# A third relu buffer, a single scratch for the maxima, and normalisations moved between the first value tiles, in a fused attention and MLP block

## The chip, the cores and the metric

One core of one Trainium2 chip runs the whole program as one launch. The metric is device time in microseconds; lower is better. A core has five engines with a queue each: TensorE (PE, its weight loads shown as PEld), VectorE (DVE), ScalarE (ACT), GpSimd (POOL) and SyncE (SP), which here only issues DMA transfers. Each engine works its queue in order, and engines wait for one another at semaphores.

## The reference

The input `x` has 2048 rows of 640. One normalisation feeds both an attention with a sliding window and an MLP with a squared relu; the MLP gates the attention.

```python
def _A_ref(x, wqkv, wo):
    H = 32; Dh = D // H; W = 256
    q, k, v = ...                      # x @ wqkv, split into 32 heads of 20
    scores = jnp.einsum("bhqd,bhkd->bhqk", q, k) * (Dh ** -0.5)
    mask = (idx[:, None] - idx[None, :] >= 0) & (idx[:, None] - idx[None, :] < W)
    p = _softmax(jnp.where(mask[None, None], scores, -1e9), axis=-1)
    o = jnp.einsum("bhqk,bhkd->bhqd", p, v)
    return o.transpose(...).reshape(B, S, D) @ wo

def _B_ref(x, w1, b1, w2, b2):         # 640 -> 1536 -> 640
    h = jnp.einsum("bsd,df->bsf", x, w1) + b1
    r = jnp.where(h > 0, h, 0)
    return jnp.einsum("bsf,fd->bsd", r * r, w2) + b2

xn = _layernorm(A_x)
return A_x + _A_ref(xn, A_wqkv, A_wo) * _silu(_B_ref(xn, ...))
```

## The kernel before, in words

Every number that is multiplied is carried as a high part and a rest ("split"), so most products are three matmuls that accumulate in one PSUM tile, and ScalarE and VectorE make the two parts.

**First phase** (about the first 117 us). The rows are worked in four blocks of 512 (four tiles of 128). For each block the x tiles are loaded on SP (`load_x`), VectorE takes mean and variance (`stats`), ScalarE takes the root and VectorE the reciprocal (`inv_std`, L146 and L147), and VectorE normalises each tile (`normalize`, L151). TensorE turns the normalised tiles (`transpose_chunks`, L167); the first heads' queries and keys and all values are multiplied out of the result. `v_all(b)` makes the values of block `b`: for each half `nh` of the 640 columns and each of four row tiles `t`, TensorE adds 15 matmuls (L230) into a tile of the pool `pmm`, which has three; ScalarE copies the high part (L254), VectorE subtracts it (L255, into `r1`, which has two buffers), and the `rest` (L258 on ScalarE, L259 on VectorE) follows one tile later. Between the two halves `next_x` turns the next block's x, and for later blocks the statistics and normalisations run as `jobs` inside `v_all`. For block 0 the order is different: the second block's normalisations and eleven transfers (the x tiles of the third block, the two spills of the first block's turned x, both biases, the ones rows and the raw weights of the second head group) stand ahead of `v_all(0)`. The order within each engine is the order in which the code calls them: the phase is under a manual schedule, as is the rest.

**Attention and MLP** (about 117 to 830 us). The loop runs 268 steps; 256 of them are one query tile of one of 16 pairs of heads. `scores` multiplies queries and keys for the pair's two heads (L439, into the PSUM tag `s`, two buffers), and `maxima` (L451) adds the mask and takes the row maximum on VectorE: one instruction for each head, whose full-size result goes into a scratch tile `junk` that nothing reads, and whose maximum goes into `mt`, read out by an accumulator instruction of its own. Every fourth step the maxima become rows (L455, L456, a turn on TensorE at L465, a copy at L469) that join the queries. Nine steps later `scores_t` (L483), `exps` (L490 on ScalarE, the window cut by POOL at L491 and L493), `high` (L498) and `low` (L504, `pl`) make the probabilities, and `values` (L518) multiplies them with the values. Between these pieces `fill` feeds TensorE with the remaining queries and keys and the MLP, planned by estimated costs. `flush` runs what the fillers left over: for each of 96 half chunks of the MLP, `half(h)` takes the relu of one half of the PSUM tile `hps` into `r` on ScalarE (L806), squares it there for the high part (L807), and lets VectorE multiply the same half of `hps` with `r` (L809, into `sq`) and POOL subtract (L810). `half(0)` runs at one flush and `half(1)` at the next. `at2` is the pool of `junk` and `r`, two buffers by default.

**The end** (about 830 us on) turns the attention's output, multiplies it with `wo` and combines it with the gate and the input.

Of the kernel before, what the change touches and what calls it, by code (L numbers as in the profile page):

```python
# [7 lines left out]
F32 = mybir.dt.float32  # L8
F32R = mybir.dt.float32r
BF16 = mybir.dt.bfloat16  # L10
# [4 lines left out]
P = 128  # L15
# [6 lines left out]
KC = D // P  # L22
# [9 lines left out]
MT = 256  # L32
# [19 lines left out]
def attn_mlp_kernel(ctx: ExitStack, tc, x, wqkv, wo, w1, b1, w2, b2, out):  # L52
# [62 lines left out]
    def ones_rows(i):  # L115
        nc.sync.dma_start(ks[i][KR:KR + 2].rearrange("a h (c n) -> a (h c) n", n=2 * P), ones.unsqueeze(1).to_broadcast([2, S // P, 2 * P]))
# [10 lines left out]
    with tc.tile_pool(name="ph1v", bufs=2) as p1v, tc.tile_pool(name="ph1", bufs=2) as p1, tc.tile_pool(name="ph1x", bufs=4) as p1b, tc.tile_pool(name="ph1w", bufs=1) as p1w:  # L127
        xts = {}

        def load_x(b, upto=4):  # L130
            xts.setdefault(b, [])
            for t in range(len(xts[b]), upto):
                xt = p1b.tile([P, D], F32, tag="xt", name=f"xt_{b}_{t}")
                nc.sync.dma_start(xt, x[(4 * b + t) * P:(4 * b + t + 1) * P, :])
                xts[b].append(xt)
# [9 lines left out]
        def inv_std(rstd, var):  # L145
            nc.scalar.activation(rstd, var, AF.Sqrt, bias=eps)  # L146
            nc.vector.reciprocal(rstd, rstd)  # L147

        def normalize(xt, mv, rstd):
            xn = p1b.tile([P, D], F32, tag="xn", name="xn")  # L150
            nc.vector.tensor_scalar(xn, xt, mv[:, 0:1], rstd, ALU.subtract, ALU.mult)  # L151
            return xn
# [5 lines left out]
        def spill_x(b):  # L158
            for p in range(2):
                nc.sync.dma_start(xs_d[p][b], f32(xT[p][b]))  # L160
# [9 lines left out]
        def load_w(raw_src, shape3=None):  # L170
            raw = wgt.tile([P, D], F32, tag="wraw", bufs=RAW, name="raw")
            if shape3:
                raw = raw.rearrange("p (c n) -> p c n", c=shape3)
            nc.sync.dma_start(raw, raw_src)
            return raw
# [53 lines left out]
            for m, (xp, wp, c) in enumerate(mms):  # L229
                nc.tensor.matmul(ps, xT[xp][b][:, c * BT + t * P: c * BT + (t + 1) * P], wv[wp][:, c, nh * HALF:(nh + 1) * HALF], start=first and m == 0, stop=not first and m == len(mms) - 1)  # L230

        def v_all(b, between=None):
            late = []
            jobs = norm_jobs(b + 2) if b + 2 < NB else []
            for nh in range(2):
                if nh and between:
                    between()
                vt = p1v.tile([P, NP // 2, 4, 2, VW], BF16, tag="vt", name="vt")
                nc.gpsimd.memset(vt[:, :, :, :, VW - 1:VW], 1.0)
                ahead = 2 if between and not nh else 1  # L240
                pss = []
                for t in range(4):
                    if t in (0, ahead) or t > ahead:
                        ts = range(t, max(t + 1, ahead))
                        for t_ in ts:
                            pss.append(pmm.tile([P, HALF], F32, tag="mm", name="vps"))
                            v_part(pss[-1], b, t_, nh, [(xp, wp, c) for c in range(KC) for xp, wp in ((0, 0), (1, 0))], True)
                        for t_, ps in zip(ts, pss):
                            v_part(ps, b, t_, nh, [(0, 1, c) for c in range(KC)], False)
                    ps = pss.pop(0)  # L250
                    psv = ps.rearrange("p (a h d) -> p a h d", a=NP // 2, h=2)
                    dst = vt[:, :, t, :, :]
                    r1 = p1.tile([P, NP // 2, 2, DH], F32, tag="r1", name="r1")
                    nc.scalar.activation(dst[:, :, :, 0:DH], psv, AF.Copy)  # L254
                    nc.vector.tensor_sub(r1, psv, dst[:, :, :, 0:DH])  # L255

                    def rest(dst=dst, r1=r1):
                        nc.scalar.activation(dst[:, :, :, DH:2 * DH], r1, AF.Copy)  # L258
                        nc.vector.tensor_sub(dst[:, :, :, 2 * DH:3 * DH], r1, dst[:, :, :, DH:2 * DH])  # L259
                    if late:  # L260
                        late.pop()()
                    late.append(rest)
                    for _ in range(0 if between and not nh else 2 if between else 1):
                        if jobs:
                            jobs.pop(0)()
                    store_all()
                late.pop()()
                stores.append((v_d[:, nh * (NP // 2):(nh + 1) * (NP // 2), b, :], vt.rearrange("p a t h w -> p a (t h w)")))

        E_ = mybir.EngineType  # L270
        with tc.manual_schedule(engines={E_.PE, E_.Activation, E_.DVE, E_.Pool, E_.SP}):
# [103 lines left out]
            for b in range(NB):  # L375
                def next_x():
                    if b + 1 < NB:
                        alloc_x(b + 1)
                        transpose_chunks(b + 1, xns)
                        xns.clear()  # L380
                        store_all()
                        spill_x(b + 1)

                if b == 0:
                    inv_std(rstd1, mv1[:, :, 1])
                    xns = [normalize(xts[1][t], mv1[:, t, :], rstd1[:, t:t + 1]) for t in range(4)]
                    load_x(2)
                    spill_x(0)
                    nc.sync.dma_start(b1t, b1.rearrange("(c p) -> p c", p=P))
                    nc.sync.dma_start(b2t, b2.partition_broadcast(P))  # L390
                    ones_rows(0)
                    raws = [load_w(group_src(1, w), KC) for w in "qk"]
                    v_all(b, next_x)
                    continue
                lasts = []
                for w in "kq":
                    ps = pmm.tile([P, BT], F32, tag="mm", name="qkps")
                    qk_group(w, b, ps)
                    lasts.append(qk_evac(w, b, ps))
                for f in lasts:  # L400
                    f()
                next_x()
                if b == 1:
                    for w in "qk":
                        ws1[w] = group_tiles(1, w)
                        split_w(*ws1[w], raws.pop(0))
                if b == NB - 1:
                    store_all()
                    for half in range(2):
                        for dst, src in pair_loads(0, half):  # L410
                            nc.sync.dma_start(dst, src)
                v_all(b)
# [32 lines left out]
    def maxima(p, q, r, nk):  # L445
        if q % 4 == 0:
            mts[p, q // 4] = at2.tile([P, 2, 4], F32, tag="mt", name="mt")
        mt = mts[p, q // 4]
        for hh in range(2):
            junk = at2.tile([P, 3 * P], BF16, tag="junk", name="junk")  # L450
            nc.vector.tensor_tensor_reduce(out=junk[:, :nk], in0=r[hh][:, :nk], in1=mask[:, 3 * P - nk:], scale=1.0, scalar=-3.0e38, op0=ALU.add, op1=ALU.max, accum_out=mt[:, hh, q % 4:q % 4 + 1])  # L451
        if q % 4 == 3:

            mp = mps[q // 4 % 2][:, 0:16].rearrange("p (h a b) -> p h a b", h=2, a=2)
            nc.vector.tensor_scalar(mp[:, :, 0, :], mt, -1.0, None, ALU.mult)  # L455
            nc.vector.scalar_tensor_tensor(mp[:, :, 1, :], mt, -1.0, mp[:, :, 0, :], ALU.mult, ALU.subtract)  # L456
            mts[p, q // 4] = mps[q // 4 % 2]
# [272 lines left out]
    def filler():  # L730
# [51 lines left out]
        for n, (hf, b) in enumerate(blocks):  # L782
# [12 lines left out]
            for fc in range(NFH):  # L795
                ps = pmm.tile([P, BT], F32, tag="mm", name="hps")
                yield from mm_group(ps, [(lin1(wt1, (wp * KC + c) * FHALF + fc * P, P), xb[xp][:, c * BT:(c + 1) * BT]) for c in range(KC) for wp, xp in ((0, 0), (0, 1), (1, 0))], 0.213)
                hh = [stg.tile([P, BT], F32R, tag="stg", name="hh"),
                      stg.tile([P, BT], F32R, tag="stg", name="hl") if fc < NFH - 4 else wgt.tile([P, D], F32R, tag=f"wg{'kq'[fc % 2]}l", name="hl")[:, :BT]]
                hs.append(hh)  # L800

                def evac(ps=ps, hh=hh, fi=hf * NFH + fc):
                    def half(h):
                        sl = slice(h * MT, (h + 1) * MT)
                        r = at2.tile([P, MT], F32, tag="relu", name="relu")
                        nc.scalar.activation(r, ps[:, sl], AF.Relu, bias=b1t[:, fi:fi + 1])  # L806
                        nc.scalar.activation(hh[0][:, sl], r, AF.Square)  # L807
                        sq = at2.tile([P, MT], F32, tag="sq", name="sq")
                        nc.vector.scalar_tensor_tensor(sq, ps[:, sl], b1t[:, fi:fi + 1], r, ALU.add, ALU.mult)  # L809
                        nc.gpsimd.tensor_sub(hh[1][:, sl], sq, f32(hh[0][:, sl]))  # L810
                    half(0)
                    late.append(lambda: half(1))
                pending.append(evac)
# [254 lines left out]
```

## Time and profile before

| | |
|---|---|
| median of 3 runs | 920.18 us (920.01 to 920.91) |
| profiled execution | 920.92 us, of which 919.2 us from the first instruction to the last |
| granted TensorE clock | 0.999 |
| busy: PE, PEld, DVE, ACT, POOL | 901.6, 728.5, 752.9, 668.6, 535.2 us |

Busy times are unions over the span, so an engine at 98% of 919.2 us is hardly ever without an instruction; matmuls overlap and their ends are modelled, so that alone doesn't say that TensorE is at its peak. The chain of waits is followed back from the last instruction: at each step to whatever released it, or to the instruction before it on the same engine. In lists in order of time, each row has the start in us from the span's start, the length, the engine and line, and in square brackets how long the engine had been idle and who released it; idle times under 0.15 us are not named there.

### The profile page before, as it was taken

The numbers are of one execution on the slowest core, as the hardware profiler recorded it, in microseconds if no ns is written. First come the engines' busy times: TensorE is split into PE (matmuls) and PEld (weight loads), VectorE is DVE, ScalarE is ACT, GpSimd is POOL, SyncE is SP. The second block draws the span as 40 slices with busy tenths as digits, with TensorE's granted clock in tenths as the row PEclk, the third lists the DMA queues.
The fourth block names the chain that finished last, engine by engine and source line by source line (L and its number), as shares of the span: only waits on it lengthen the run. The fifth ranks groups of instructions, "written<-read, shape, count | busy, mean of one in ns | idle before, by whom it ended". The sixth has DMA issues, their size and how long they took to land.

```text
span 919.2 us, 21779 instructions
## 1 busy us (share of the span) xinstructions
PE 901.6 (98%) x7632; PEld 728.5 (79%) x7632; DVE 752.9 (82%) x2031; ACT 668.6 (73%) x1282; POOL 535.2 (58%) x832
## 2 busy tenths in 40 slices
PE   9999999999999999999999999999999999999998
PEld 8999976666666678688688788678788687789998
DVE  7875478989899988988888989987888988875654
ACT  5454339888988986987986988977987977994221
POOL 6010017887778885775765877875864965872000
PEclk9999999999999999999999999999999999999999
DMA  6899786677877453253255144365174264055873
GB/s 240 287 396 333 219 264 203 220 221 233 266 232 243 134 197 98 88 182 119 70 184 166 53 123 151 102 226 158 51 252 134 74 208 145 19 191 188 285 276 115
DMA packets 130803, 168.79 MB, mean 184 GB/s; under 512 B 44100, under 2 KB 91268, under 8 KB 128132
## 3 DMA queue, kind: packets, MB, share of 16 engines
q1 hardware_dynamic: 130692, 167.39, 56.2%
q8 instruction: 60, 0.98, 0.4%
q14 instruction: 51, 0.42, 0.1%
HBM read 96.15 MB, written 70.91 MB: 182 GB/s over the span
## 4 chain that ended last, share of the span: by engine, by line
PE 76%; DVE 12%; ACT 5%; issue 3%; POOL 3%; DMA 1%; DVEq 0%; POOLq 0%; SPq 0%; ACTq 0%
PE yps L851 16%; PE hps L569 14%; PE wops L569 8%; PE vps L230 7%; PE ops L518 7%; PE stps L483 7%; PE sps L439 7%; PE qkps L569 6%; DVE junk L451 3%; DVE pl L504 3%; PE qkps L200 2%; ACT p L490 2%; DVE w L672 1%; ACT ph L498 1%; PE otp L917 1%
## 5 line engine op out<-in xcount | busy, mean ns | idle before, releaser
L490 ACT ACTIVATE p<-stps,ebias 128x384 f32<-128x384 f32 (+2 forms) x512 | 258.3, 557 | 80.7 <-PE stps L483 67.3
L451 DVE CUSTOM_DVE_ANT_0 junk<-sps,mask 128x384 bf16<-128x384 f32 (+2 forms) x512 | 250.9, 526 | 59.1 <-PE sps L439 51.9
L504 DVE TENSOR_TENSOR pl<-p,ph 128x768 f16<-128x768 f32 (+2 forms) x256 | 243.1, 950 | 3.4 <-ACT ph L498 3.3
L491 POOL TENSOR_SCALAR_AFFINE_SELECT p<-p 128x256 f32<-128x256 f32 x256 | 146.1, 571 | 127.7 <-ACT p L490 117.5
L498 ACT ACTIVATE ph<-p 128x768 f16<-128x768 f32 (+2 forms) x256 | 206.0, 805 | 14.1 <-POOL p L493 11.7
L569 PE MATMUL hps<-xb,w 128*128 128x512 f32 x630 | 198.2, 430 | 0.0
L851 PE MATMUL yps<-w,hh 128*128 128x320 f32 x768 | 197.6, 330 | 0.0
L851 PEld LDWEIGHTS yps<-w,hh 128*128 128x128 f32 x768 | 132.2, 189 | 7.8 <-issue 1.6
L569 PEld LDWEIGHTS hps<-xb,w 128*128 128x128 f32 x630 | 113.3, 189 | 21.5 <-issue 0.7
L439 PE MATMUL sps<-ks,qs 120*128 120x384 bf16 (+2 forms) x512 | 127.5, 319 | 2.4 <-DVE mt L451 1.9
L483 PE MATMUL stps<-qs,ks 122*128 122x384 bf16 (+2 forms) x512 | 124.5, 322 | 3.6 <-ACT p L490 1.9
L851 PE MATMUL yps<-w,hl 128*128 128x320 f32 x384 | 126.6, 330 | 0.0
L810 POOL TENSOR_TENSOR hl<-sq,hh 128x256 fp32r<-128x256 f32 x96 | 102.6, 1070 | 37.4 <-DVE sq L809 25.2
L493 POOL TENSOR_SCALAR_AFFINE_SELECT p<-p 128x256 f32<-128x256 f32 x224 | 112.4, 502 | 0.0
L518 PEld LDWEIGHTS <-ph 128*128 128x128 f16 x1440 | 86.0, 97 | 26.4 <-issue 21.5
L518 PE MATMUL ops<-vp,ph 128*128 128x61 bf16 x1440 | 101.0, 192 | 0.0
L518 PE MATMUL ops<-vp,pl 128*128 128x61 bf16 x1440 | 99.7, 191 | 0.0
L518 PEld LDWEIGHTS <-pl 128*128 128x128 f16 x1440 | 87.8, 97 | 0.0
L851 PEld LDWEIGHTS yps<-w,hl 128*128 128x128 f32 x384 | 72.4, 189 | 4.6 <-issue 1.5
L483 PEld LDWEIGHTS <-ks 122*128 122x128 bf16 x512 | 30.0, 99 | 56.4 <-issue 44.9
L230 PE MATMUL vps<-wv,xT 128*128 128x320 f32 x480 | 71.7, 308 | 0.6 <-DVE r L255 0.6
L230 PEld LDWEIGHTS vps<-wv,xT 128*128 128x128 f32 x480 | 70.5, 188 | 0.9 <-DVE r L255 0.9
(116 smaller groups left out, 1476.9 us busy)
## 6 DMA issues: line engine op xcount, KB each, us to landing
ks<-k_d SPq DMA_DIRECT2D x64, 240.0 KB
qs<-q_d SPq DMA_DIRECT2D x64, 240.0 KB
xb<-xs SPq DMA_DIRECT2D x12, 1280.0 KB
xs<-xT SPq DMA_DIRECT2D x8, 1280.0 KB
y<-ysb SPq DMA_DIRECT2D x32, 320.0 KB
q_d<-shm SPq DMA_DIRECT2D x38, 256.0 KB
v_d<-vt SPq DMA_DIRECT2D x8, 976.0 KB
vp<-v_d SPq DMA_DIRECT2D x16, 488.0 KB
```

The source lines that it names most:

```text
L230: nc.tensor.matmul(ps, xT[xp][b][:, c * BT + t * P: c * BT + (t + 1) * P], wv[wp][:, c, nh * HALF:(nh + 1) * HALF], start=first and m == 0 ...
L439: nc.tensor.matmul(ps[:, :nk], qs[i][0:KR, hh, q * P:(q + 1) * P], ks[i][0:KR, hh, k0 * P:k0 * P + nk], start=True, stop=True)
L451: nc.vector.tensor_tensor_reduce(out=junk[:, :nk], in0=r[hh][:, :nk], in1=mask[:, 3 * P - nk:], scale=1.0, scalar=-3.0e38, op0=ALU.add, op ...
L483: nc.tensor.matmul(ps[:, :n], ks[i][0:KR + 2, hh, kb * P:(kb + 1) * P], qs[i][0:KR + 2, hh, kb * P:kb * P + n], start=True, stop=True)
L490: nc.scalar.activation(p32[:, hh, :n], r[hh][:, :n], AF.Exp, scale=SCALE, bias=ebias)
L491: nc.gpsimd.affine_select(p32[:, :, 0:P], p32[:, :, 0:P], pattern=[[0, 2], [1, P]], compare_op=ALU.is_ge, fill=0.0, base=0, channel_multip ...
L493: nc.gpsimd.affine_select(p32[:, :, 2 * P:], p32[:, :, 2 * P:], pattern=[[0, 2], [-1, P]], compare_op=ALU.is_gt, fill=0.0, base=0, channel ...
L498: nc.scalar.activation(ph[:, :, :n], p32[:, :, :n], AF.Copy)
L504: nc.vector.tensor_sub(pl[:, :, :n], p32[:, :, :n], ph[:, :, :n])
L518: nc.tensor.matmul(ot[:, q % 4, hh, :], t[:, hh, (q - k) * P:(q - k + 1) * P], vp[:, k // 4, k % 4, hh, :], start=m == 1, stop=m == 2 * le ...
L569: nc.tensor.matmul(ps, a, b_, start=j == 0, stop=j == n - 1)
L851: nc.tensor.matmul(pss[nh], hs[fc][hp][:, tt * P:(tt + 1) * P], lin1(wt2, (wp * NFH + fc) * D + nh * HALF, HALF), start=fc == 0 and j == 0 ...
```

## The change

Three edits. The scratch `junk` of the maxima gets one buffer instead of two. The relu `r` gets three instead of two. And in block 0 the second block's normalisations no longer stand ahead of `v_all(0)`: the root, the reciprocal and the first two tiles come behind the first value tile's copy and subtraction, the third tile behind the second value tile's, and the fourth, with the eleven transfers, behind the third's.

```diff
-        def v_all(b, between=None):
+        def v_all(b, between=None, firsts=()):
...
                     if late:
                         late.pop()()
                     late.append(rest)
+                    if not nh and t < len(firsts):
+                        firsts[t]()
...
                 if b == 0:
-                    inv_std(rstd1, mv1[:, :, 1])
-                    xns = [normalize(xts[1][t], mv1[:, t, :], rstd1[:, t:t + 1]) for t in range(4)]
-                    load_x(2)
-                    spill_x(0)
-                    nc.sync.dma_start(b1t, b1.rearrange("(c p) -> p c", p=P))
-                    nc.sync.dma_start(b2t, b2.partition_broadcast(P))
-                    ones_rows(0)
-                    raws = [load_w(group_src(1, w), KC) for w in "qk"]
-                    v_all(b, next_x)
+                    xns, raws = [], []
+
+                    def norm1(t0, n):
+                        if t0 == 0:
+                            inv_std(rstd1, mv1[:, :, 1])
+                        for t in range(t0, t0 + n):
+                            xns.append(normalize(xts[1][t], mv1[:, t, :], rstd1[:, t:t + 1]))
+
+                    def loads1():
+                        load_x(2)
+                        spill_x(0)
+                        nc.sync.dma_start(b1t, b1.rearrange("(c p) -> p c", p=P))
+                        nc.sync.dma_start(b2t, b2.partition_broadcast(P))
+                        ones_rows(0)
+                        raws.extend(load_w(group_src(1, w), KC) for w in "qk")
+                    v_all(b, next_x, [lambda: norm1(0, 2), lambda: norm1(2, 1), lambda: (norm1(3, 1), loads1())])
                     continue
...
-            junk = at2.tile([P, 3 * P], BF16, tag="junk", name="junk")
+            junk = at2.tile([P, 3 * P], BF16, tag="junk", bufs=1, name="junk")
...
-                        r = at2.tile([P, MT], F32, tag="relu", name="relu")
+                        r = at2.tile([P, MT], F32, tag="relu", bufs=3, name="relu")
```

## The prediction

> **What bounds the kernel now.** First the page: which engine is full, and through what the chain of work that ended last runs.
>
> ```profile
> PE 901.6 (98%) x7632; PEld 728.5 (79%) x7632; DVE 752.9 (82%) x2031; ACT 668.6 (73%) x1282; POOL 535.2 (58%) x832
> PE 76%; DVE 12%; ACT 5%; issue 3%; POOL 3%; DMA 1%; DVEq 0%; POOLq 0%; SPq 0%; ACTq 0%
> ```
>
> TensorE sets the time over most of the span, but 12% of the chain is VectorE. Second view: how the chain splits by line (the head of the chain listed in order of time), and the row of the maxima, L451, in the view of their tile.
>
> ```profile
> by line: PE yps L851 16.3%; PE hps L569 13.7%; PE wops L569 7.7%; PE vps L230 7.0%; PE ops L518 6.8%; PE stps L483 6.7%; PE sps L439 6.6%; PE qkps L569 6.5%; DVE junk L451 3.5%; DVE pl L504 2.8%; issue 2.7%; PE qkps L200 2.5%; ACT p L490 1.
> L451 DVE CUSTOM_DVE_ANT_0 junk<-sps,mask x512: 275/552/561, 119.5 to 806.9; 128x384 bf16<-128x384 f32 x149, 128x128 bf16<-128x128 f32 x11, 128x256 bf16<-128x256 f32 x11
> ```
>
> The maxima are 512 instructions, a pair for each of 256 attention steps. 3.5% of 919.2 us is 32 us of them on the chain. The steps lie in 806.9 - 119.5 = 687 us, so one step is 2.69 us and a stretch of 25 us has 9.3 of them. Third view: busy time by engine in stretches of 25 us (columns: stretch, length, PE, PEld, DVE, ACT, POOL busy). The first eight are the attention stretches where VectorE has least room; the ninth is the fullest of all others.
>
> ```profile
> 142.00:167.00 25.00, 25.00 (x196) 17.37 (x195) 23.34 (x66) 22.14 (x41) 19.44 (x27) 1.00 0.68 210
> 167.00:192.00 25.00, 24.24 (x209) 16.53 (x208) 23.79 (x61) 21.65 (x42) 21.06 (x29) 1.00 0.68 216
> 217.00:242.00 25.00, 23.64 (x209) 16.20 (x208) 23.30 (x61) 21.02 (x40) 19.71 (x29) 1.00 0.76 233
> 242.00:267.00 25.00, 24.59 (x208) 16.90 (x204) 23.63 (x63) 23.11 (x43) 19.31 (x29) 1.00 0.78 242
> 267.00:292.00 25.00, 23.96 (x208) 16.36 (x208) 24.56 (x60) 21.82 (x41) 20.71 (x28) 1.00 0.67 210
> 292.00:317.00 25.00, 23.27 (x199) 15.63 (x196) 24.86 (x65) 22.47 (x45) 20.29 (x27) 1.00 0.58 174
> 542.00:567.00 25.00, 24.69 (x251) 21.64 (x251) 24.86 (x68) 19.82 (x35) 18.24 (x27) 1.00 0.58 166
> 567.00:592.00 25.00, 24.83 (x216) 17.09 (x215) 23.66 (x67) 23.40 (x48) 19.36 (x28) 1.00 0.40 120
> ...
> 717.00:742.00 25.00, 24.98 (x216) 18.30 (x213) 22.84 (x64) 23.27 (x48) 23.46 (x36) 1.00 0.34 100
> ```
>
> In three of them (24.56, 24.86, 24.86) VectorE is full and TensorE is not: there VectorE sets the pace, and what is added to it is added to the kernel. The granted clock is 1.00 in all of them, so no term below comes from the clock.
>
> **Edit 1: one scratch buffer for the maxima.** Nothing is added to compute; `junk` is written and never read. With two buffers the two heads of a step write different ones. With one, the second head's maxima overwrites the first's, and the order of two writes to one buffer has to be kept by a wait of VectorE for itself. What the pair looks like now (start, length):
>
> ```profile
> 401.23 0.55 DVE L451 CUSTOM_DVE_ANT_0 junk<-sps,mask 128x384 bf16<-128x384 f32 x1
> 401.70 0.08 DVE L451 DVE_READ_ACCUMULATOR2_ANT mt<- 128x1 f32 x1
> 401.70 0.55 DVE L451 CUSTOM_DVE_ANT_0 junk<-sps,mask 128x384 bf16<-128x384 f32 x1
> ```
>
> The second starts 0.08 us before the first has ended (401.78): unordered neighbours overlap. What a wait of VectorE for its own last instruction costs is seen where a buffer already comes round. First the chain of waits at `srt`, which has two buffers: its third writer follows the first one's reader, L211.
>
> ```profile
> 19.56 0.65 DVE slo L211
> 20.21 0.03 issue
> 20.24 0.02 DVEq L207
> 20.26 0.05 issue
> 20.31 0.43 DVE srt L207
> ```
>
> 0.10 us pass from the end of L211 to the start of L207, with an item of VectorE's sequencer (DVEq) between. The same for `r1`, two buffers, third writer L255 behind the first one's reader L259; ScalarE's input was there at 26.90.
>
> ```profile
> 26.47 0.43 ACT L254 ACTIVATE vt<-vps 128x320 bf16<-128x320 f32 x1
> 26.60 0.50 DVE L259 TENSOR_TENSOR vt<-r,vt 128x320 bf16<-128x320 f32 x1 [0.15 <-ACT vt L258]
> 27.20 0.49 DVE L255 TENSOR_TENSOR r<-vps,vt 128x320 f32<-128x320 f32 x1
> ```
>
> Again 0.10 us (27.10 to 27.20). Both instructions have a second thing to wait for, as a maxima has (its scores). The cheaper form, one wait alone, is L455 behind the maxima:
>
> ```profile
> 406.65 0.09 DVE L451 DVE_READ_ACCUMULATOR2_ANT mt<- 128x1 f32 x1
> 406.76 0.17 DVE L455 TENSOR_SCALAR mp<-mt 128x8 bf16<-128x8 f32 x1
> ```
>
> 0.02 us here. So a pair grows by 0.08 of lost overlap plus 0.10, that is 0.18 us; the lower end with a wait is 0.08 + 0.02, taken as 0.11 with the 0.01 of rounding; the lowest is nothing, if no wait is set. A gain is excluded: the instructions stay the same. I take 0.18, since the maxima has two waits like L207 and L255. The first maxima of a step would wait for the second one of the step before, but `pl` (L504) and more lie between, so that wait is met when it is reached: nothing. Behind the waiting instruction on VectorE stand `mp`, the copy of the rows, the splits and `pl`; TensorE waits for the scores' bank that a maxima frees and for `mp`.
>
> How much of 0.18 x 256 = 46 us shows? Where TensorE paces, the step has room and it is hidden; that cover ends where VectorE's busy time nears the full stretch. From below: 32 us of maxima on the chain are 31 pairs of 1.02 us (twice 0.55 less the overlap of 0.08), and 31 x 0.18 = 5.6 us are added to a chain that can only get longer. By stretches: each gets 9.3 x 0.18 = 1.67 us more, and what then exceeds 24.6 of 25 (the least of the three full ones) prolongs it, by 1.67 at most: 0.4, 0.9, 0.4, 0.7, 1.6, 1.7, 1.7, 0.7, in the order of the rows, 8.0 us with the hundredths. The ninth row comes to 24.5 and stays hidden. I take 8.0, because it also counts stretches that fill up only by the change; ends 0 and 46.
>
> **Edit 2: a third buffer for the relu.** No instruction is added or removed. ScalarE writes `r` (L806), then reads it (L807); VectorE reads it (L809). All that a further buffer could take away is ScalarE's wait for L809:
>
> ```profile
> ACT relu L806 <- DVE sq L809: 1.7, 6, 0.5
> 330.92 0.47 ACT L806 ACTIVATE relu<-hps,b1t 128x256 f32<-128x256 f32 x1
> 331.82 0.48 DVE L809 SCALAR_TENSOR_TENSOR sq<-hps,b1t,relu 128x256 f32<-128x256 f32 x1
> 332.34 0.47 ACT L806 ACTIVATE relu<-hps,b1t 128x256 f32<-128x256 f32 x1 [0.50 <-DVE sq L809]
> ```
>
> 1.7 us in six waits. But look at whom the second L806 waits for: the L809 that ends at 332.30 reads the half before, which sits in the other of two buffers. The buffer that is written at 332.34 was last read a whole chunk earlier. So the buffer is not what it waits for; what both share is the tile `hps`, of which each reads its half. I take 0, ends 0 and -1.7. The Trainium skill, "PSUM — Partial Sum Buffer", section "PSUM bank collisions raise a hardware error", says that ScalarE and VectorE must not read one bank at the same time and that compilers therefore order any two such accesses. By that rule the wait stays with any number of buffers (0), by the buffer reading 1.7 us go; the row fits the rule.
>
> **Edit 3: the second block's normalisations between the first value tiles.** Moved: one root (L146) on ScalarE, one reciprocal and four L151 on VectorE, and on SP eleven transfers (four x tiles, two spills, both biases, the ones rows, two raw weights). POOL gets and loses nothing.
>
> ```profile
> 22.98 0.81 ACT L254 ACTIVATE vt<-vps 128x320 bf16<-128x320 f32 x2
> 23.47 2.18 DVE L151 TENSOR_SCALAR xn<-xt,mv,rstd 128x640 f32<-128x640 f32 x4
> 25.57 0.88 DVE L255 TENSOR_TENSOR r<-vps,vt 128x320 f32<-128x320 f32 x2
> 18.73 6.76 PE L230 MATMUL vps<-wv,xT 128*128 128x320 f32 x45
> 26.11 2.47 PE L230 MATMUL vps<-wv,xT 128*128 128x320 f32 x15 [0.61 <-DVE r L255]
> 28.42 2.34 PE L167 MATMUL tps<-ident,xn 128*128 128x128 f32 x20
> 26.94 1.81 SPq L134 DMA_DIRECT2D xt<-in_A_x_dram  x4
> 39.41 1.80 SPq L174 DMA_DIRECT2D raw<-in_A_wqkv_dram  x2
> 50.80 0.77 ACT L178 ACTIVATE wgqh<-raw 128x640 fp32r<-128x640 f32 x1
> ```
>
> TensorE stands for 0.61 us before the fourth value tile, since the first tile's bank is freed by an L255 that queues behind all four L151. Now the first L255 can go once its L254 is through, at about 23.3, and ends about 23.8, long before TensorE needs the bank at 25.49: the gap goes, -0.6. What is late next: the transposes need the last L151. VectorE from 23.8: reciprocal 0.2, two L151 1.1, L255 0.5, L259 0.5, L151 0.6, L255 and L259 1.0 gives the last L151 from about 27.1 to 27.7; TensorE ends the fourth tile at 25.49 + 2.3 = 27.8. Just covered; should it be late by some tenths, the gap comes back in front of L167, so -0.6 to 0. SP: the x loads start at 26.94 behind stores; the last of four needs its buffer from the last L151 and would go at 26.94 + 3 x 0.45 = 28.3, later than 27.7, so nothing shifts, and the raw weights issued at 39.41 are not split before 50.80. From 26.11 to the end of this phase TensorE runs without such a gap, so 0.6 us arrives at the end. I take -0.6.
>
> **Sum.** +8.0 + 0 - 0.6 = +7.4 us. The profiled execution took 920.92 us (span 919.2, the rest around it 1.7), 0.74 above the median of 920.18. On the profiled one: 928.3; for the median 927.6, which I give.
>
> **The rivals.** *The order costs nothing.* Either no wait is set for two writes on one in-order engine, or it is free. Then only -0.6 is left: 919.6, no change. For it: 225 of the 256 pairs are not on the chain; against it, the two gaps of 0.10 us above. It decides from a price per pair of about 0.08 us down: 9.3 x 0.08 = 0.74 in each of the three full stretches is 2.2, and with -0.6 it stays under 1.8. The Trainium skill, "VectorE: DVE Perf Modes", section "The DRAIN you can't avoid", has measured that a semaphore after every copy "costs nothing extra", because the next instruction waits for the pipe anyway; by it 919.6 comes out here. This trace disagrees: neighbours start 0.08 us before the end, waiting ones 0.10 after.
>
> *The cheap wait.* 0.11 us a pair, 1.02 a stretch: the same eight rows give 0, 0.2, 0, 0.1, 1.0, 1.0, 1.0, 0.1, in all 3.4, less 0.6: 923.0.
>
> *The relu pays and the maxima don't.* -1.7 - 0.6 from edits 2 and 3, place: ScalarE's six waits in the MLP chunks: 917.9. Against it: whom L806 waits for, and that ScalarE is 5% of the chain.
>
> *The wait is paid everywhere.* If the scores' banks and `mp` come late in every step, up to 46 - 0.6: 965.6. Against it: outside the eight stretches VectorE has 2.2 us or more of room in 25, by the ninth row.
>
> **How the numbers follow.** Forecast (925 to 936) 0.55; cheap wait (922 to 925) 0.20; no cost (918.4 to 922) 0.13; faster 0.04; paid far more widely (above 936) 0.08. About 0.2%, 1.8 us, is what a measurement of this kernel can tell from no change; so slower 0.83, same 0.13, faster 0.04. The range takes in the no-cost case and leaves out the last two: 919.4 to 936. The likeliest case has 925 to 936 for itself.
>
> **What would show it.** In the changed trace the pair's starts lie 0.65 us apart instead of 0.47 (0.58 with the cheap wait, 0.47 with none); stretches around 270 to 320 and 545 to 570 grow while those where TensorE paces keep their step of about 2.7 us; L806 still waits for L809 about six times; and TensorE's row at 26.11 has lost its 0.61. The prediction falls if the pair's starts stay at 0.47, or if TensorE's slack takes in more than I gave it.

## The result and the profile after

The changed kernel takes 934.23 us (median of 6 runs, 933.95 to 935.24) against 920.17 us before (6 runs, 919.87 to 920.91): ratio 1.0152, 95% interval 1.0142 to 1.0162. It is 14.1 us slower, where +7.4 was predicted. The profiled execution has a span of 932.5 us at a granted clock of 1.00.

The page of the kernel after: the span, the engines' busy times, and the shares of its chain by engine.

```profile
span 932.5 us, 22164 instructions
PE 904.7 (97%) x7632; PEld 729.2 (78%) x7632; DVE 767.8 (82%) x2031; ACT 671.0 (72%) x1282; POOL 541.7 (58%) x832
PE 52%; DVE 7%; ACT 4%; issue 2%; POOL 1%; DMA 0%; SPq 0%; DVEq 0%; POOLq 0%; ACTq 0%
```

The instructions are as many as before on every engine. The chain's shares sum to 66%: it breaks off in the middle of the attention, so nothing is read from it here. VectorE's timeline of one pair of maxima (start, length):

```profile
283.98 0.55 DVE L460 CUSTOM_DVE_ANT_0 junk<-sps,mask 128x384 bf16<-128x384 f32 x1
284.46 0.08 DVE L460 DVE_READ_ACCUMULATOR2_ANT mt<- 128x1 f32 x1
284.68 0.56 DVE L460 CUSTOM_DVE_ANT_0 junk<-sps,mask 128x384 bf16<-128x384 f32 x1
```

The starts lie 0.70 us apart, not 0.48 as before. The first pair member is over at 284.54 with its accumulator read, the second starts 0.14 later. The view of the maxima's line has one more new row (length least/median/most in ns): items of VectorE's own sequencer. Before there were four of them:

```profile
L451 DVEq EVENT_SEMAPHORE  x4: 50/50/232, 118.9 to 119.2; - x4
```

After:

```profile
L460 DVEq EVENT_SEMAPHORE  x389: 21/21/234, 118.5 to 820.0; - x195
```

Each of the 256 second maxima now has such an item ahead of it. The other 133 belong to first maxima and, all but two, are over 0.3 us or more before these start (1.25 us, median), so they hold nothing up.

Over all 256 pairs the mean distance of the starts is 0.684 us after and 0.455 before: the price of the wait is 0.229 us. Next the views of waits (who waits for whom: us in total, times, longest). Before:

```profile
DVE junk L451 <- PE sps L439: 51.9, 89, 1.8
PE sps L465 <- DVE mp L456: 3.6, 6, 1.5
PE sps L439 <- DVE mt L451: 1.9, 8, 0.6
```

After:

```profile
DVE junk L460 <- PE sps L448: 23.7, 49, 1.6
PE sps L448 <- DVE mt L460: 10.3, 23, 1.0
PE sps L474 <- DVE mp L465: 6.3, 11, 1.5
ACT relu L815 <- DVE sq L818: 4.3, 7, 1.1
```

VectorE's waiting for scores halves (28 us less), and TensorE stands 8.4 us longer before the next scores, whose bank a maxima has to free, and 2.7 us longer before the turned maxima. Last the busy times by stretch. The 256 steps fall into four stretches: steps 0 to 87, 88 to 151, 152 to 183 and 184 to 255 (columns as in the prediction). Before:

```profile
120.00:355.00 235.00, 228.63 (x1871) 161.70 (x1869) 214.72 (x578) 196.66 (x362) 175.24 (x247) 1.00 0.70 217
355.00:526.00 171.00, 170.80 (x1580) 133.24 (x1577) 146.75 (x436) 139.59 (x272) 117.73 (x200) 1.00 0.39 124
526.00:616.00 90.00, 87.31 (x803) 68.41 (x802) 83.52 (x233) 78.23 (x150) 70.45 (x102) 1.00 0.47 141
616.00:806.00 190.00, 189.98 (x1745) 148.87 (x1744) 162.18 (x482) 154.23 (x301) 130.91 (x222) 1.00 0.42 133
```

After, the same steps:

```profile
119.00:363.00 244.00, 231.15 (x1875) 162.87 (x1874) 219.59 (x582) 198.22 (x362) 175.71 (x248) 1.00 0.67 209
363.00:534.00 171.00, 170.90 (x1577) 133.07 (x1576) 149.94 (x436) 139.75 (x272) 122.05 (x199) 1.00 0.40 124
534.00:629.00 95.00, 88.28 (x803) 68.39 (x801) 87.59 (x232) 78.16 (x148) 67.83 (x103) 1.00 0.45 138
629.00:819.00 190.00, 189.62 (x1742) 148.53 (x1741) 165.63 (x481) 154.61 (x300) 134.69 (x219) 1.00 0.42 130
```

The reader is to see the first two numbers of each row. In the second and the fourth stretch TensorE was busy all the time before (0.2 us idle in 361), and these stretches keep their length although each of their pairs is longer. In the first and the third TensorE already stood for 6.4 and 2.7 us, and these two grow by about 8 and 5 us. Measured from the ends of the second maxima, the growth is 8.1, -0.1, 5.2 and 0.3 us. The third number of each row marks the same two stretches: before, VectorE was busy for 91% and 93% of them, for 86% and 85% of the others.

### The profile page after: what moved, and what is told of

The parts are those of the page before. It is cut to its first block, busy times and chain, and to the rows that moved or that the text cites. A ratio compares the mean times of both kernels' runs of the same rounds, so it can differ in the third digit from the quotient of the medians.

```text
span 932.5 us, 22164 instructions
## 1 busy us (share of the span) xinstructions
PE 904.7 (97%) x7632; PEld 729.2 (78%) x7632; DVE 767.8 (82%) x2031; ACT 671.0 (72%) x1282; POOL 541.7 (58%) x832
## 4 chain that ended last, share of the span: by engine, by line
PE 52%; DVE 7%; ACT 4%; issue 2%; POOL 1%; DMA 0%; SPq 0%; DVEq 0%; POOLq 0%; ACTq 0%
PE yps L860 15%; PE hps L578 12%; PE wops L578 8%; PE ops L527 5%; PE stps L492 5%; PE sps L448 5%; DVE pl L513 2%; DVE junk L460 2%; ACT p L499 1%; DVE w L681 1%; ACT ph L507 1%; PE otp L926 1%; DVE sq L818 1%; ACT relu L815 1%; POOL p L500 0%
## 5 line engine op out<-in xcount | busy, mean ns | idle before, releaser
L460 DVE CUSTOM_DVE_ANT_0 junk<-sps,mask 128x384 bf16<-128x384 f32 (+2 forms) x512 | 270.7, 529 | 65.0 <-PE sps L448 23.7
L500 POOL TENSOR_SCALAR_AFFINE_SELECT p<-p 128x256 f32<-128x256 f32 x256 | 157.1, 614 | 121.5 <-ACT p L499 105.1
L819 POOL TENSOR_TENSOR hl<-sq,hh 128x256 fp32r<-128x256 f32 x96 | 105.7, 1102 | 43.8 <-DVE sq L818 29.7
L502 POOL TENSOR_SCALAR_AFFINE_SELECT p<-p 128x256 f32<-128x256 f32 x224 | 107.0, 478 | 0.0
```

The costliest lines, as they stand in the source:

```text
L500: nc.gpsimd.affine_select(p32[:, :, 0:P], p32[:, :, 0:P], pattern=[[0, 2], [1, P]], compare_op=ALU.is_ge, fill=0.0, base=0, channel_multip ...
L502: nc.gpsimd.affine_select(p32[:, :, 2 * P:], p32[:, :, 2 * P:], pattern=[[0, 2], [-1, P]], compare_op=ALU.is_gt, fill=0.0, base=0, channel ...
```

## The experiments

The theory at this point: the single scratch costs 0.229 us of VectorE's time per pair, and it shows only in the two stretches where VectorE was fullest and TensorE had idle time already. The rivals: another edit contributes; the loss is spread over all steps; a wait costs more than its time; or only the place counts, because the second maxima frees the bank that TensorE waits for. "Price" below is the mean distance of a pair's starts less the 0.455 us of before, and "exposed" is the loss divided by 256 times the price.

**Each edit by itself.** The scratch alone, on the kernel before:

```
-            junk = at2.tile([P, 3 * P], BF16, tag="junk", name="junk")
+            junk = at2.tile([P, 3 * P], BF16, tag="junk", bufs=1, name="junk")
```

> Edit 1 alone on the kernel before: one scratch buffer, relu and normalisations as before. Theory W (VectorE's wait for its own last maxima makes the whole loss): starts of a pair 0.70 us apart, +14 to +15 us (about 934.7), since edit 3 is no longer there to give back 0.6. Rival M (the loss comes from the three edits together, the relu's third buffer or the moved transfers among them): clearly less than +14, about half.

Measured: 935.89 us against 920.25, ratio 1.0177 (1.0162 to 1.0193), +15.6 us, price 0.229. The scratch makes the whole loss.

The other two edits without it. Three relu buffers leave no room for the second scratch, so the tile of ones that fills the keys' extra rows was made smaller (2 x 64 instead of 2 x 256, read more often by its transfers):

```
-    ones = const.tile([2, 2 * P], BF16, name="ones")
+    ones = const.tile([2, P // 2], BF16, name="ones")
...
-            junk = at2.tile([P, 3 * P], BF16, tag="junk", bufs=1, name="junk")
+            junk = at2.tile([P, 3 * P], BF16, tag="junk", name="junk")
```

> Edits 2 and 3 without edit 1: three relu buffers, normalisations moved, two scratch buffers. To make room the ones rows are kept as 64 columns instead of 256 and spread by the transfer. Theory W: 919.3 to 919.8, that is -0.4 to -0.9 us (edit 3), pair starts 0.48 us apart, and as many ScalarE waits of the relu for sq as before (about six). If the relu's buffer pays: 917.9 (-2.3) and none of those waits. Rival M: a loss of several us stays.

Measured: 920.51 us, ratio 1.0003 (0.9994 to 1.0012): no difference from before. The view of the relu's tile, with three buffers, has for the wait of the relu for `sq`

```profile
  DVE sq L818: 1.7, 6
```

which is before's 1.7 us in six waits to the digit. The third buffer takes none of them away.

The moved normalisations alone (the first two hunks of the diff, on the kernel before):

> Edit 3 alone on the kernel before. Theory of the prediction: TensorE's 0.6 us gap before the fourth value tile goes and arrives at the end, -0.6 us. Rival: the gap goes, but the attention has a stretch that waits for transfers (steps 40 to 56 in the run without edit 1 took back 1.1 us of a late start), so that an early start is lost there: -0.2 to +0.2 us.

Measured: 920.03 us, ratio 0.9993 (0.9984 to 1.0002). TensorE's timeline, where 26.11 had its gap of 0.61 us:

```profile
19.05 8.96 PE L230 MATMUL vps<-wv,xT 128*128 128x320 f32 x60
27.85 2.35 PE L167 MATMUL tps<-ident,xn 128*128 128x128 f32 x20
...
64.05 2.47 PE L230 MATMUL vps<-wv,xT 128*128 128x320 f32 x15 [0.41 <-DVE r L255]
```

The gap is gone, all 60 matmuls run on, but one of 0.41 us stands at 64.05, where before there was none. It waits for an L255, and VectorE reaches that one late, since ahead of it in its queue the statistics (L142) wait for the fourth block's x tiles. SP's transfers of these and VectorE's first two statistics on them, from the timeline, before:

```profile
45.01 4.92 SPq L134 DMA_DIRECT2D xt<-in_A_x_dram  x4
55.31 0.89 DVE L142 BATCH_NORM_STATS2 st<-xt 128x6 f32<-128x320 f32 x2 [0.21 <-DMA xt<-in_A_x_dram]
```

and here, with the x tiles of the third block ahead of them (26.94 before):

```profile
27.26 1.90 SPq L134 DMA_DIRECT2D xt<-in_A_x_dram  x4
45.79 4.27 SPq L134 DMA_DIRECT2D xt<-in_A_x_dram  x4
57.44 0.89 DVE L142 BATCH_NORM_STATS2 st<-xt 128x6 f32<-128x320 f32 x2 [2.90 <-DMA xt<-in_A_x_dram]
```

The transfers are issued 0.3 and 0.8 us later, and the statistics start 2.1 us later. Most of what was gained at 26 us is lost again at 64; why the tiles land later by more than they were issued later stays open. This does not happen in every kernel with the moved normalisations. Of the five traces with them, two have the gap at 64 us: this one, and that of the three relu buffers with two scratches (0.99 us). The changed kernel has neither gap: from its first statistics to its first maxima it takes 114.9 us, against 115.7 before and 115.7 in this run.

**How the price is made up, and whether the loss follows it.** The changed kernel with the heads' maxima in the other order:

```
-        for hh in range(2):
+        for hh in (1, 0):
```

> The changed kernel, but the maxima are taken of the second head first. VectorE then has already waited for the later of the two score tiles when it comes to the second maxima, which waits for its own engine alone, without an item of the sequencer ahead of it. Theory W with the price by form: starts of a pair 0.57 to 0.59 us apart (0.08 lost overlap and 0.02 to 0.04 of wait), +3 to +5 us over the kernel before. If the loss goes in proportion to the price (0.11 of 0.23 us): about +6.5. If any wait for its own engine costs the same: +14.

Measured: 928.07 us, ratio 1.0087 (1.0073 to 1.0100), +7.8 us. The pair, and the sequencer's items:

```profile
281.59 0.55 DVE L460 CUSTOM_DVE_ANT_0 junk<-sps,mask 128x384 bf16<-128x384 f32 x1
282.07 0.08 DVE L460 DVE_READ_ACCUMULATOR2_ANT mt<- 128x1 f32 x1
282.18 0.56 DVE L460 CUSTOM_DVE_ANT_0 junk<-sps,mask 128x384 bf16<-128x384 f32 x1
```

```profile
L460 DVEq EVENT_SEMAPHORE  x4: 49/50/232, 118.6 to 118.9; - x4
```

The items are back at four, and the second maxima starts 0.03 us after the accumulator read instead of 0.14. Head 1's scores are issued last; a maxima that comes second and reads head 0's has them for certain, and one wait is left, for VectorE itself. With two things to wait for, the sequencer gets an item of its own ahead of the instruction. The price is 0.114, half, and so is the loss: exposed are 7.8 / (256 x 0.114) = 0.27, and with the scratch alone 15.6 / (256 x 0.229) = 0.27. For the changed kernel the same sum gives 0.24; the intervals of the times leave 0.02 to 0.04 either way, so these three are hardly told apart. The loss came nearest to the expectation that it goes in proportion to the price (+6.5); +3 to +5 is ruled out (6.7 to 9.2 by the interval).

**Where it shows.** The kernel before with one scratch in the first and third stretch (120 steps), two in the others:

```
+    scratch = at2.tile([P, 2, 3 * P], BF16, tag="junk", bufs=1, name="junk")
...
-            junk = at2.tile([P, 3 * P], BF16, tag="junk", name="junk")
-            nc.vector.tensor_tensor_reduce(out=junk[:, :nk], ...
+            nc.vector.tensor_tensor_reduce(out=scratch[:, 0 if p * NT + q < 88 or 152 <= p * NT + q < 184 else hh, :nk], ...
```

> The kernel before, with the two heads' maxima sharing one scratch in 120 of the 256 steps only: steps 0 to 87 and 152 to 183, where VectorE is fullest; in the other 136 steps each head has its own. Theory W with cover (the wait shows only where VectorE has no room): nearly the whole loss, +12 to +14.5. If each pair pays the same wherever it is: 120/256 of 14.6, that is +6.8.

Measured: 935.11 us, ratio 1.0165 (1.0151 to 1.0178), +14.9 us. The complement, one scratch in the other 136 steps (`not (...)` in the same line):

> The complement: the two heads share one scratch in the 136 steps 88 to 151 and 184 to 255 only, where TensorE set the pace. Theory W with cover: 0 to +1.5 us, though pair starts are 0.70 us apart in all of these steps. If each pair pays the same: 136/256 of 16, that is +8.5.

Measured: 921.19 us against 920.67, ratio 1.0007 (0.9998 to 1.0016). The row of the maxima in it, for the last start at 807.1 (before 806.9):

```profile
L451 DVE CUSTOM_DVE_ANT_0 junk<-sps,mask x512: 276/552/560, 119.9 to 807.1; 128x384 bf16<-128x384 f32 x149, 128x128 bf16<-128x128 f32 x11, 128x256 bf16<-128x256 f32 x11
```

The price is paid there too (mean start distance 0.684 in those 136 steps), 31 us of VectorE's time in all, and by the interval at most 1.5 us of it arrive. The 120 steps make 95% of the loss.

**No scratch at all.** The changed kernel, its maxima writing over the scores that they have read:

```
-            nc.vector.tensor_tensor_reduce(out=junk[:, :nk], in0=r[hh][:, :nk], ...
+            nc.vector.tensor_tensor_reduce(out=r[hh][:, :nk], in0=r[hh][:, :nk], ...
```

> The changed kernel without any scratch: the maxima write their full-size result over the score tile that they read, which nothing reads afterwards. Theory W: no two maxima share a buffer, so no wait of VectorE for itself, pair starts as before (0.48 us), time 919.5 to 920.5, the whole loss gone with edits 2 and 3 kept. Rival: writing to PSUM makes a maxima longer; each 0.05 us of it, twice a step, would cost 0.1/0.225 of 16 us, that is +7.

Measured: 923.12 us against 920.67, ratio 1.0026 (1.0016 to 1.0036). The start distance is before's (mean 0.454), so five sixths of the loss go with the order; but 2.5 us stay, where none were expected. What differs is the accumulator read, 0.14 us for 0.08:

```profile
L459 DVE DVE_READ_ACCUMULATOR2_ANT mt<- x512: 128/140/149, 120.4 to 810.1; 128x1 f32 x171
```

That this makes the 2.5 us is likely, and was not tried by itself.

**Is it the wait, or the time?** The kernel before with work between the two maxima of a pair instead of a wait. First an addition of two 128x128 pieces of the mask:

```
+    idle = at2.tile([P, P], F32, tag="idle", bufs=1, name="idle")
...
+            if hh:
+                nc.vector.tensor_add(idle, mask[:, 0:P], mask[:, P:2 * P])
```

> The kernel before with two scratch buffers, and in each step one addition of 128x128 on VectorE between the two maxima, to a tile of its own that nothing reads; by the sizes of the additions in the trace it should move the second maxima by about 0.23 us, as the wait does. Theory W (it is 0.23 us of VectorE ahead of the second maxima that costs, whatever fills it): +14 to +17 us. If it is the wait itself (the sequencer, the semaphore) that harms: clearly less.

Measured: 951.73 us, ratio 1.0336 (1.0320 to 1.0352), +31 us. The dose was not the one meant: its row runs from 273 to 1247 ns.

```profile
L453 DVE TENSOR_TENSOR idle<-mask x256: 273/357/1247, 119.7 to 837.6; 128x128 f32<-128x128 f32 x128
```

So two small multiplications (128x8) were tried in the same place, and, in another kernel, behind `pl`:

```
+    def tiny():
+        for j in range(2):
+            nc.vector.tensor_scalar(idle[j], mask[:, 0:8], -1.0, None, ALU.mult)
```

> The kernel before, with two scratch buffers, and two small VectorE multiplications (128x8, result unused, the form of L455) between the two maxima of every step: no wait is added, the second maxima comes later by the two operations' time (an estimate from L455, 0.11 us from the start of one such operation to the next: 0.2 to 0.25 us). Theory A (time of VectorE lost ahead of the second maxima is what costs, whatever fills it): 70 pair-equivalents x 0.2 to 0.25, 934 to 938. Theory B (the wait itself costs more than its time, for instance because it stops VectorE's sequencer from reading ahead): clearly less than the single scratch, 920 to 927.

> The kernel before, and the same two small multiplications after pl (L504) instead, as often as there are pairs. Theory A1 (the second maxima is what must not be late, since TensorE stands before the next scores until it has freed their bank; work elsewhere finds slack): well below the kernel with the operations between the maxima, 920 to 927. Theory A2 (VectorE's time alone counts, it is full in the steps concerned, and the place does not matter): the same as with the operations between the maxima, within 2 us, 932 to 938.

Measured: 946.32 us (1.0274, 1.0260 to 1.0288) between the maxima, 964.99 us (1.0477, 1.0463 to 1.0492) after `pl`. Both theories on record missed, since these operations too are long at times, and longer behind `pl`:

```profile
L436 DVE TENSOR_SCALAR idle<-mask x512: 151/160/1155, 145.0 to 876.3; 128x8 f32<-128x8 f32 x171
```

The last pair took a small maxima of 8 columns of the mask, of the maxima's own kind:

```
+    def tiny():
+        nc.vector.tensor_tensor_reduce(out=idle, in0=mask[:, 0:8], in1=mask[:, P:P + 8], scale=1.0, scalar=-3.0e38, op0=ALU.add, op1=ALU.max, accum_out=idlem[:, 0:1])
```

> The kernel before, with two scratch buffers, and one small maxima (8 columns of the mask, result unused) between the two maxima of every step. It takes the place of the multiplications of the two kernels with small work, which were held up by GpSimd's instructions and so had no steady size; estimate of its time from those rows, 0.16 to 0.25 us, no wait added. If time of VectorE is what counts, it costs 0.25 to 0.35 of its total (256 x its time), as the multiplications did: 931 to 943. If a wait costs more than work of the same length, clearly less than the single scratch at the same length: under 928.

> The kernel before, and the same small maxima after pl (L504) instead. If the place does not matter (VectorE's time counts, wherever it is taken), the same as with it between the maxima, within 2 us. If the second maxima is what must not be late, 5 us or more below that.

Measured: 939.51 us (1.0206, 1.0192 to 1.0220) between the maxima, 955.80 us (1.0384, 1.0370 to 1.0398) after `pl`. The work was not steady either, so "the same within 2 us" failed as well: 16 us lie between the two, but so does a dose of 0.23 against 0.42 us. The doses were therefore taken from the traces: between the maxima the mean start distance less 0.455, behind `pl` the mean time from the end of `pl` to the end of the added work. All of them side by side:

| added to VectorE in each step | mean, us | loss, us | loss / (256 x mean) |
|---|---|---|---|
| one wait (heads swapped, changed kernel) | 0.114 | 7.8 | 0.27 |
| wait with its sequencer item (scratch alone) | 0.229 | 15.6 | 0.27 |
| small maxima between | 0.231 | 19.1 | 0.32 |
| two multiplications between | 0.296 | 25.4 | 0.33 |
| addition between | 0.344 | 31.1 | 0.35 |
| small maxima after `pl` | 0.418 | 35.4 | 0.33 |
| two multiplications after `pl` | 0.497 | 44.0 | 0.35 |

The doses of the second and third row agree on average only. The small maxima took 0.32 us a step in the first stretch and 0.18 to 0.20 in the others; the wait took 0.22 to 0.23 everywhere. By stretch, 0.44 of the wait and 0.45 of the small maxima came through in the first, 0.69 and 0.59 in the third. A wait costs about what work of the same length costs; a tenth of the share either way is not resolved.

Whether the place matters stays open. Summed over the span, a microsecond behind `pl`, far from the second maxima, costs as much as between the maxima. But where the wait shows, the shares are 0.4 to 0.5 behind `pl` and 0.45 to 0.6 between the maxima, at doses and with instructions that are not the same. What evens out the totals is that the larger doses fill the stretches that had room. For the small maxima after `pl` the growth by stretch is 15.8, 7.7, 4.8 and 6.2 us; its row of the second one, 88 to 151:

```profile
371.00:550.00 179.00, 174.71 (x1586) 134.50 (x1585) 170.76 (x566) 142.76 (x276) 120.25 (x201) 1.00 0.38 119
```

VectorE is busy for 95% of it (86% before), and TensorE, busy throughout before, now stands for 4.3 us.

No version beat the kernel before: the moved normalisations alone, at 0.07% less, cannot be told from it.

## Why the prediction was right or wrong

**Direction and place: right.** The wait appears, VectorE waits for itself, the first maxima of a step does not pay, and the loss lies in the stretches named (270 to 320 and 545 to 570 among them), while the steps paced by TensorE keep theirs (2.67 us in steps 88 to 151, before and after). "Costs nothing", "the relu pays" and "paid everywhere" are out: 14.1 us of a possible 58.6 came through. The page of the Trainium skill quoted for "costs nothing", "VectorE: DVE Perf Modes", section "The DRAIN you can't avoid", states a measurement on copies that does not hold for these maxima: even the single wait of the swapped heads costs 0.114 us a pair, since the neighbour that waits for nothing starts before the other has ended.

**Size, first term: the price.** "0.08 of lost overlap plus 0.10, that is 0.18" should have been 0.229. The 0.08 was right; the 0.10, taken over from L207 and L255, was not. In the trace after, the sequencer's item starts 0.04 us behind the accumulator read, takes 0.02, and the maxima starts 0.08 behind the item: 0.144 in all, the median of the 256 pairs. L207 and L255 start 0.05 and 0.04 behind their items. In the kernel before, no maxima but the very first waits for VectorE itself, so no row of it had the 0.144; the prediction took over the 0.10 without room for another kind of instruction. The prediction's own stretch sum with 9.3 x 0.229 = 2.13 us in place of 1.67 gives 0.9, 1.3, 0.8, 1.2, 2.1, 2.1, 2.1, 1.2 and, for the ninth row, 0.4: 12.1 instead of 8.0. So about 4 of the 6.6 us that were missed are the price.

**Size, second term: how much of it shows.** "What then exceeds 24.6 of 25" took VectorE as the bound only where it is nearly full, and 44 pairs' worth came out (8.0 / 0.18). Measured were 62 to 68 (14.1 and 15.6 over 0.229, 7.8 over 0.114), as many at half the price as at the full one. A cover that runs out gives fewer at the half: the same sum at 0.114 (1.06 us a stretch) is 3.6 us where 7.8 were measured, and at 0.229 it is 12.1 where the scratch alone cost 15.6. The step that failed is that nothing shows below the line at 24.6 of 25, that is 98%: stretches in which VectorE was busy for 91% (first) and 93% (third) let through 41% and 70% of the wait, and 41% and 79% at half the price; those with 86% and 85% let through nothing of it. TensorE's idle time marks the same two stretches, but it is not needed for the loss. Steps 161 to 168 before and after:

```profile
550.80:571.90 21.10, 21.10 (x213) 17.64 (x212) 20.58 (x58) 16.87 (x31) 15.38 (x22) 1.00 0.50 150
559.80:582.90 23.10, 22.06 (x212) 17.78 (x212) 21.81 (x58) 16.93 (x31) 14.00 (x22) 1.00 0.44 138
```

TensorE never stood there before, VectorE was busy for 98%, and these eight steps grow by 2.0 us: all of the 1.8 us that eight waits add came through. Over the 31 groups of eight steps the growth in the changed kernel goes more closely with VectorE's free time before (correlation -0.72) than with TensorE's idle time before (0.37). Why stretches with 7% to 9% of free time still pass on a fixed part of the wait stays open. The 31 pairs on the chain were a lower end, as stated, and too low by half. Price and share were both too small, and 934.2 lies just inside the likeliest case (925 to 936): that the case held the time owes more to its width than to the sum.

**Edit 2: right,** 0 us, by the reason given: with three buffers and nothing else slower the relu waits for `sq` as often and as long (in the changed kernel seven times, 4.3 us). That both read one PSUM tile, and the rule of the Trainium skill, "PSUM — Partial Sum Buffer", section "PSUM bank collisions raise a hardware error", fit this; no run took the shared tile away.

**Edit 3: its gap right, its -0.6 us not certain to stay.** "So nothing shifts" for SP is wrong: the x loads did shift, the fourth block's statistics waited longer for theirs, and in two of five traces this made TensorE stand at 64 us. In the changed kernel's trace TensorE did not stand there, and 0.8 us are gained by the first maxima. Whether the gain stays hung on when the transfers landed, which the prediction had put at no shift. In the time, -0.07% (-0.16 to +0.02) for the edit alone tells -0.6 us neither from nothing nor from twice as much.

**The rivals.** The "cheap wait" exists, with 0.114 us instead of 0.11, but in another kernel: the one with the heads swapped. Its time was put at 923.0 and came out at 928.1, by the second term.

## What to carry to other kernels

A second buffer for a result that nobody reads can be worth having: two writers of one buffer on one engine are ordered, and what that costs depends on how many things the second writer already waits for. Price such a wait from a row of the same kind of instruction behind the same kind of wait, and where there is none, give the price more room. Judge where it shows by the free time of the engine that waits, in short stretches, and do not take it as hidden until that engine is full: here stretches with VectorE busy for 91% and 93% let through some 40% and 70% of the wait, those with 85% nothing until larger doses had used up its room. A gap closed early in an in-order program can open again further on if the transfers behind the moved instructions go out later.

## What the runs showed of the hardware

A small VectorE operation on data in SBUF can be held up until GpSimd's running instruction is over. In the kernel with the small maxima after `pl`, GpSimd's instruction and VectorE's, from the timeline:

```profile
284.18 0.80 POOL L497 TENSOR_SCALAR_AFFINE_SELECT p<-p 128x256 f32<-128x256 f32 x1 [2.17 <-DMA q_d<-slo]
284.63 0.37 DVE L436 CUSTOM_DVE_ANT_0 idle<-mask 128x8 bf16<-128x8 f32 x1
```

One ends at 284.98, the other at 285.00; undisturbed, the same operation takes 0.15 us. Of the 512 multiplications after `pl` 229 were longer than 0.25 us, and every one of them ended 0.02 to 0.03 us after a GpSimd instruction did; so did all 120 of those between the maxima, and the 217 and 152 small maxima over 0.20 us ended 0.01 to 0.03 us after one. The kernel's own maxima, which read their scores from PSUM, show nothing of the kind (561 ns at most of 512). Not every small operation is held: 30 of the 283 short multiplications after `pl` lie inside a GpSimd instruction by the trace, whose spans for GpSimd are rough. The Trainium skill, "SBUF — State Buffer", section "SBUF: two separate sides", describes it: VectorE and GpSimd share a pair of ports, whoever comes first holds it for a whole instruction, and an operation with two inputs from SBUF needs it against a GpSimd instruction that reads SBUF, as does one in a mode that uses two ports. The traces agree for the small maxima and for the addition, of which 157 of 158 over 0.29 us ended 0.14 to 0.16 us after a GpSimd instruction; the multiplication has one input and was held up as well, and no run here shows in which mode it ran.

The other two: with its full-size result in PSUM, the maxima's accumulator read took 0.14 us instead of 0.08, and a wait for two things instead of one added 0.11 us to VectorE's next maxima.
